# Two units of the first token group's first product by seven products on summed factors, with the factor sums and attention steps placed anew

## The chip, the core and the metric

The kernel runs on one core of a Trainium2 chip. The metric is the device time of one execution in microseconds (us). Engines are named as in the profile: PE multiplies matrices (PEld is its loading of the stationary operand), DVE and ACT work on elements, POOL and SP issue DMAs here. Each engine works through its own instructions in order and waits for others by semaphores.

## The reference

A linear attention with decay, in blocks of 64 positions, over 4 batches, 8 heads, 768 positions and 64 dimensions, feeds a two-layer network. Its result is laid out as 3072 tokens of 512 values.

```python
intra = np.einsum('bhic,bhjc->bhij', qb, kb) * Dmask[None]
intra = np.einsum('bhij,bhjd->bhid', intra, vb)
inter = np.einsum('bhid,bhde->bhie', qb * lam_pow[None], kv_state)
out[:, :, sl] = intra + inter
kv_state = lam_block[None, :, None, None] * kv_state + np.einsum('bhsd,bhse->bhde', kb_dec, vb)
...
h = x @ w_in             # (3072, 512) @ (512, 2048)
g = h - np.tanh(h)
return (g @ w_out).astype(np.float32)   # (3072, 2048) @ (2048, 512)
```

The weights arrive as 64-bit floats. The kernel reads their two 32-bit halves and rounds them to 32 bits itself.

## The kernel before

**Tiling.** Tokens come in six groups g = 0 to 5 of 512 (128 positions of each batch). For each group the kernel makes the attention output (tiles xt, held transposed, in two halves of 256 tokens: half 0 from batches 0 and 1, half 1 from batches 2 and 3), multiplies by w_in ("up"), applies h - tanh(h), and multiplies by w_out ("down"). The hidden width of 2048 is split into four units u = 0 to 3 of 512; `w1[u]` holds the weights of a unit, in four blocks of 128 x 512. The result of a unit, 512 hidden values by 512 tokens, has four quadrants named 11, 12, 21, 22: the first digit is the half of the hidden values, the second the half of the tokens.

**Two ways to make a unit of up.** `up_plain(u, cs)` (line 954) makes quadrants directly: per quadrant 4 x 2 matmul calls, 32 per unit, each quadrant in a PSUM bank of its own (tags ya, yb, z, w), then a tanh on ACT (L971) and a subtraction on DVE (L972). `up(g, u, n)` (line 545) makes product n of a seven-product scheme (that of Strassen in Winograd's form) for the whole unit: 4 calls a product, 28 a unit. The products use sums of weights, made by `sums_in(u)` (four DVE instructions, into `ws[u]`, one into `w1[u]` itself, L261), and sums of tokens, made by `att_sums(g)` (four DVE instructions, L513 to L516). Three banks hold partial results: y takes products 1, 6, 7 and 4 one upon the other, and ACT copies y out after 1 (into bank w, L568), after 6 (L572) and after 7 (L574); w takes product 2; z takes 5 and 3. Group 0 is made by `up_plain` in all four units, groups 1 and on by products (from group 2 on, in a form with a further level).

**The order.** A scheduler at compile time orders the instructions of each engine: earliest in the program first, among those that its own model of times finds ready. `tied(yes, op)` (line 125) pins an instruction behind the one traced just before it on its engine. In between, untied instructions can move ahead of earlier ones that are not ready. PE's plain matmuls are tied in unit 0 and between the parts `att_inter` and `att_intra` (`held["yes"]`). `sums_in` is tied.

**The first 145 us.** Group 0's attention and the weights of the first units come first. Each weight block of 512 KB is loaded by SP, rounded by three ACT instructions (L291 to L293) and two DVE instructions (L295, L296). `weights(n)` sees to it that n blocks are rounded: 16 blocks of w_in, then 16 of w_out, two for each kt = 0 to 7. Then come the four plain units, with the attention of group 1 put between quadrants by the list `turns` (line 1058) in pieces: `att_transpose`, `att_scores`, `att_state`, `att_inter`, `att_intra`, once for batches 0 and 1 (`p0`), once for 2 and 3 (`p1`). `att_intra` waits for a small ACT copy named "seen" (L486) that follows `att_inter`. The loop over kt (line 1081) is the down product of group 0, in seven products of two calls each, into seven banks `acc`, with `sums_out` (sums of w_out, stored to DRAM by POOL for the later groups), `sums_late` and three `sums_in` placed in it. `sums_first(u)` makes two sums of hidden values that this loop reads for unit u = kt // 2. For every third kt the pair of weight tiles of w_out is lent from `ws` (`pair_tiles`, line 249), where no sums of weights are held yet. `powers` (line 108) makes decay factors that attention from group 1 on needs. `first_results` ends group 0; line 1113 begins group 1 with product 1 of its unit 0.

Of the kernel before, what the change touches and what calls it, by code (L numbers as in the profile page):

```python
# [24 lines left out]
def kernel(  # L25
# [32 lines left out]
    nc = tc.nc  # L58
# [190 lines left out]
    def pair_tiles(kt):  # L249

        if kt % 3 == 2:
            return tuple(ws[u].rearrange("p x k c -> p (x k) c")[:, 0:4] for u in (3, 2))
        wt = wst.tile([128, 8, 256], F32, name="wt", tag="w")
        return wt[:, 0:4], wt[:, 4:8]
# [157 lines left out]
    def att_state(g, bs):  # L412
# [17 lines left out]
        for p in range(NP):  # L430
            nc.scalar.activation(mid[:, :, p], old[:, :, p], AF.Copy, scale=fwd[:, p, HALF - 1:HALF])
# [77 lines left out]
    def att_sums(g, bs):  # L509
        x0, x1 = xt[g, 0], xt[g, 1]  # L510
        b11, b21, b12, b22 = x0[:, 0:2], x0[:, 2:4], x1[:, 0:2], x1[:, 2:4]
        tt = xpool.tile([128, 3, 2, HB], F32, name="tt", tag="tt")
        nc.vector.tensor_tensor(tt[:, 0], b12, b11, op=AL.subtract)  # L513
        nc.vector.tensor_tensor(tt[:, 1], b22, tt[:, 0], op=AL.subtract)
        nc.vector.tensor_tensor(b12, b22, b12, op=AL.subtract)
        nc.vector.tensor_tensor(tt[:, 2], b21, tt[:, 1], op=AL.subtract)  # L516
        xt[g] = dict(B11=b11, B21=b21, B22=b22, T1=tt[:, 0], T2=tt[:, 1], T3=b12, T4=tt[:, 2])
# [12 lines left out]
    def product_bank(key, n):  # L530
# [3 lines left out]
        if n == 5 or n == 2 and key[0] == "down":  # L534
            banks[key, "zw"[n == 2]] = bank("zw"[n == 2], "zw"[n == 2], 1)
# [9 lines left out]
    def up(g, u, n):  # L545
# [6 lines left out]
        for m in range(2):  # L552
            for kt in range(2):
                nc.tensor.matmul(out=t[:, m, :], lhsT=wt[:, kt, ts(m, 128)], rhs=x[:, kt, :],  # L554
                                 start=first and m == 0 and kt == 0, stop=kt == 1, skip_group_check=True)
# [10 lines left out]
        if n == 1:  # L566
            w = banks[key, "w"] = bank("w", "w", 1)
# [386 lines left out]
    def up_plain(u, cs):  # L954

        hm = {}
        for c in cs:
            a, t = divmod(c - 11, 10)
            hm[c] = bank("h", ("ya", "yb", "z", "w")[2 * t + a], 1).rearrange("q (m c) -> q m c", m=2)
# [19 lines left out]
    def sums_first(u):  # L979
        g11, g12, g22, s1 = (hidden(0, c)[:, u] for c in (11, 12, 22, "S1"))  # L980
        nc.vector.tensor_tensor(s1, g12, g22, op=AL.add)
        nc.vector.tensor_tensor(g12, g11, g12, op=AL.subtract)
# [42 lines left out]
    for b in (0, 1):  # L1025
# [28 lines left out]
    weights(2 * KI)  # L1054
    every(up_plain(0, (12, 22)))
    sums_first(0)
    p0, p1 = attention(1)
    turns = [(1, 11, 2, ()), (1, 21, 2, ()), (1, 12, 2, ()), (1, 22, 2, ()), (2, 11, 0, ()), (2, 21, 1, p0[0:1]),
             (3, 11, 0, p0[1:3]), (3, 21, 1, p0[3:4]), (2, 12, 1, p0[4:]), (2, 22, 1, p1[0:1]), (3, 12, 1, p1[1:3]),
             (3, 22, 1, ())]  # L1060
    for u, c, n, more in turns:
        every(up_plain(u, (c,)))
        ahead = (u, c) == (2, 12)
        if ahead:
            run(more)
        weights(ready["done"] + n, u > 1)
        if not ahead:
            run(more)
        if c == 22:
            sums_first(u)  # L1070
            if u == 1:
                ready["to"] = len(blocks)
                load(B + 2)
                load_weights(NU * KI + 2)
                load(B + 3)
                load_weights(NU * KI + WAHEAD)
                load(2 * B)
                powers()
    sums_out(0)
    weights(NU * KI + 6, True)  # L1080
    for kt in range(KH):
        down_first(kt, (1, 2))
        if kt == 0:
            run(p1[3:4])
            down_first(kt, (5,))
            run(p1[4:])
        if kt + 1 < KH:
            sums_out(kt + 1)
        sums_late(kt)
        down_first(kt, (4, 7, 6, 3) if kt == 0 else (5, 4, 7, 6, 3) if kt + 1 < KH else (5, 6, 7, 4, 3))  # L1090
        if kt + 3 < KH:
            weights(ready["done"] + 2)
        if kt in (1, 4, 6):
            sums_in((1, 4, 6).index(kt))
# [177 lines left out]
```

## Time and profile before

| | us |
|---|---|
| median of three timed runs | 649.97 |
| the three | 647.11, 649.97, 650.4 |
| the profiled execution | 646.58 |
| its span, first to last instruction | 644.8 |

| engine | busy us | share of the span | instructions |
|---|---|---|---|
| PE | 635.1 | 98% | 6440 |
| DVE | 478.2 | 74% | 948 |
| ACT | 268.0 | 42% | 620 |
| POOL | 229.0 | 36% | 397 |

Lines of the profile name the engine, the line of the kernel, the operation, what is written from what, and shapes. "x16" is a number of instructions; one matmul call in the program is two PE instructions in the trace. A bracket at the end of a line of the timeline is the idle time of that engine just before, with the instruction that ended it. Times are us from the start of the span. In lists of waits the columns are the total, the number and the longest.

### The profile page before, as it was taken

How to read it: one execution, taken by the hardware profiler on the slowest of the kernel's cores; microseconds unless marked ns; L12 is line 12 of the kernel's file. 1: busy time of each engine (PE TensorE's matmuls, PEld its weight loads, DVE VectorE, ACT ScalarE, POOL GpSimd, SP SyncE). 2: the span in 40 equal slices, each digit the busy share in tenths (PEclk: the TensorE clock that was granted, in tenths of full speed). 3: DMA queues.
4: the chain of work that ended last, by engine and by line, in shares of the span. 5: the costliest groups of instructions: out<-in, count | busy, mean ns of one | idle time of the engine just before them, and what ended most of it. 6: DMA issues, size and time to landing. Idle time of an engine off the chain costs nothing.

```text
span 644.8 us, 16628 instructions
## 1 busy us (share of the span) xinstructions
PE 635.1 (98%) x6440; PEld 583.6 (91%) x6440; DVE 478.2 (74%) x948; ACT 268.0 (42%) x620; POOL 229.0 (36%) x397
## 2 busy tenths in 40 slices
PE   8899999999999999999999999999999999999998
PEld 6788878888888999998999998999998899998997
DVE  4577597785888877579968579987668987467953
ACT  3799576503432422345331337233245332334310
POOL 0000355735443454411455430355321254521261
PEclk9999999999999999999999999999999999999999
DMA  9999988969765999884889976798883477732384
GB/s 216 233 244 232 294 265 268 348 187 267 210 164 126 288 278 298 224 188 112 230 236 304 280 203 157 184 276 249 253 198 80 138 234 241 248 105 77 100 296 145
DMA packets 166190, 139.80 MB, mean 217 GB/s; under 512 B 136864, under 2 KB 138016, under 8 KB 166112
## 3 DMA queue, kind: packets, MB, share of 16 engines
q0 software_dynamic: 31792, 104.62, 50.0%
q1 hardware_dynamic: 134176, 34.12, 25.9%
q8 instruction: 51, 0.84, 0.5%
q14 instruction: 27, 0.22, 0.1%
q10 hardware_dynamic: 144, 0.00, 0.0%
HBM read 111.94 MB, written 26.74 MB: 215 GB/s over the span
## 4 chain that ended last, share of the span: by engine, by line
PE 65%; issue 18%; POOL 8%; DVE 3%; DMA 3%; ACT 2%; SPq 2%; POOLq 0%; DVEq 0%
PE plain L849 10%; PE acc L993 7%; PE h L964 7%; PE y L906 6%; PE y L697 6%; PE zw L906 4%; PE y L554 4%; POOL wb L795 4%; PE z L697 3%; PE zs L619 2%; PE z L554 2%; PE y L619 2%; POOL wb L792 2%; PE op L501 1%; PE w L697 1%
## 5 line engine op out<-in xcount | busy, mean ns | idle before, releaser
L795 POOL DMA_DIRECT2D wb<-fine x133 | 71.8, 541 | 157.5 <-PE plain L849 107.8
L849 PE MATMUL plain<-wb,g 128*128 128x256 f32 x416 | 96.0, 381 | 0.0
L849 PEld LDWEIGHTS plain<-wb,g 128*128 128x128 f32 x416 | 77.5, 190 | 10.4
L964 PE MATMUL h<-xt,w 128*128 128x256 f32 x256 | 57.9, 382 | 1.8 <-DVE w L296 1.8
L798 POOL DMA_DIRECT2D wb<-factors x64 | 34.6, 541 | 69.2 <-PE z L697 47.9
L910 ACT ACTIVATE q<-y 128x128 f32<-128x128 f32 x76 | 21.1, 278 | 86.1 <-PE y L906 85.0
L964 PEld LDWEIGHTS h<-xt,w 128*128 128x128 f32 x256 | 47.7, 190 | 9.0 <-DVE w L296 2.0
L906 PE MATMUL y<-wb,g 128*128 128x128 f32 x336 | 44.8, 278 | 0.0
L792 POOL DMA_DIRECT2D wb<-fine_in x60 | 32.6, 545 | 29.3 <-PE z L697 11.0
L600 ACT ACTIVATE th<-g 128x512 f32<-128x512 f32 x48 | 29.5, 628 | 29.0 <-DVE g L625 28.9
L906 PEld LDWEIGHTS y<-wb,g 128*128 128x128 f32 x336 | 40.7, 192 | 0.7
L688 ACT ACTIVATE g<-y 128x512 f32<-128x512 f32 x24 | 14.3, 597 | 63.1 <-PE y L697 63.1
L404 ACT ACTIVATE k_nat<-k_nat,mask 128x64 f32<-128x64 f32 (+1 forms) x128 | 35.1, 338 | 0.6 <-DMA k_nat<-in_k_dram 0.6
L993 PE MATMUL acc<-wt,g 128*128 128x256 f32 x144 | 32.9, 380 | 0.2 <-DVE g L972 0.2
L601 DVE TENSOR_TENSOR g<-g,th 128x512 f32<-128x512 f32 x48 | 32.2, 687 | 0.4
L697 PE MATMUL z<-tt,wb 128*128 128x128 f32 x256 | 31.9, 275 | 0.0
L993 PEld LDWEIGHTS acc<-wt,g 128*128 128x128 f32 x144 | 27.2, 190 | 4.3 <-DVE g L972 0.6
L619 PE MATMUL y<-xt,w 128*128 128x256 f32 x128 | 30.3, 379 | 0.0
L619 PE MATMUL zs<-xt,ws 128*128 128x256 f32 x128 | 30.2, 379 | 0.0
L906 PE MATMUL zw<-wb,g 128*128 128x128 f32 x224 | 30.2, 278 | 0.0
L697 PEld LDWEIGHTS z<-tt,wb 128*128 128x128 f32 x256 | 30.2, 192 | 0.0
L292 ACT ACTIVATE r<-raw 128x512 int16<-128x512 uint32 x32 | 25.0, 782 | 8.3 <-DMA raw<-in_moe_w_out_dram 3.8
(236 smaller groups left out, 1476.2 us busy)
## 6 DMA issues: line engine op xcount, KB each, us to landing
wb<-fine POOLq DMA_DIRECT2D x133, 256.0 KB, 4.0
wb<-factors POOLq DMA_DIRECT2D x64, 256.0 KB, 4.3
wb<-fine_in POOLq DMA_DIRECT2D x60, 256.0 KB, 4.8
v_nat<-in_v_dram SPq DMA_DIRECT2D x24, 256.0 KB, 5.3
raw<-in_moe_w_out_dram POOLq DMA_DIRECT2D x12, 512.0 KB, 5.7
k_nat<-in_k_dram SPq DMA_DIRECT2D x20, 256.0 KB, 4.6
fine<-wt POOLq DMA_DIRECT2D x17, 256.0 KB, 3.4
raw<-in_moe_w_in_dram SPq DMA_DIRECT2D x8, 512.0 KB, 5.2
```

The source lines that it names most:

```text
L404: tc.keep_in_program_order(nc.scalar.activation(k_h, k_h, AF.Copy, scale=mask[0:rows, h % 2, h // 2, HALF - 1:HALF]))
L554: nc.tensor.matmul(out=t[:, m, :], lhsT=wt[:, kt, ts(m, 128)], rhs=x[:, kt, :], start=first and m == 0 and kt == 0, stop=kt == 1, skip_gro ...
L601: nc.vector.tensor_tensor(dst(c), src, th, op=AL.subtract)
L619: nc.tensor.matmul(out=t[:, m, :], lhsT=wt[:, kt, ts(m, 128)], rhs=x[:, kt, :], start=False, stop=kt == 1, skip_group_check=True)
L697: nc.tensor.matmul(out=dst[:, ts(u, 128)], lhsT=a, rhs=b, start=(x in (1, 5) or x == 2 and not filled) and u == 0, stop=True, skip_group_c ...
L792: nc.gpsimd.dma_start(out=t.rearrange("p m c -> p (m c)"), in_=fine_in[INNER.index(n_[1]), (5, 6, 3).index(x_)].rearrange("p u c -> p (u c)"))
L795: nc.gpsimd.dma_start(out=t.rearrange("p m c -> p (m c)"), in_=fine[TWICE.index(n_), SUB.index(x_)].rearrange("p u c -> p (u c)"))
L798: nc.gpsimd.dma_start(out=t, in_=factors[XAT[FACT[n_][1]]][:, 2 * x_:2 * x_ + 2, :])
L849: tied(held["yes"], nc.tensor.matmul(out=t[:, m, :], lhsT=a[:, u, kt, ts(m, 128)], rhs=wb[:, kt, :], start=first and u == 0 and m == 0 and ...
L906: tied(held["yes"], nc.tensor.matmul(out=dst, lhsT=a[:, u, :], rhs=wb[:, ts(u, 128)], start=x in (1, 2) and u == 0, stop=u == NU - 1, skip ...
L964: tied(u == 0 or held["yes"], nc.tensor.matmul(out=hm[c][:, m, :], lhsT=w1[u][:, i, a, ts(m, 128)], rhs=xt[0, t][:, i, :], start=m == 0 an ...
L993: tied(held["yes"], nc.tensor.matmul(out=acc[n][:, r, :], lhsT=a[:, ts(r, 128)], rhs=b, start=kt == 0 and r == 0, stop=kt == KH - 1, skip_ ...
```

## The change

In group 0, units 1 and 2 are made by seven products; units 0 and 3 stay plain. Around it:

- `att_sums(0)` runs before unit 0's second two quadrants. Since the plain units still read the tokens, its third sum T3 is written to a free place among the hidden sums (unit 3's part of S1), and unit 3's `sums_first` moves from its last quadrant to kt = 3.
- `sums_in(1)` and `sums_in(2)` move from kt = 4 and 6 to before and into unit 1, and `sums_in(0)` from kt = 1 to kt = 6. The pair tiles lent are now those of units 3 and 0.
- Unit 1's products come one after the other (1, 5, 2, 6, 7, 4, 3), all tied on PE, its banks z and w taken from the four of attention. Unit 2's products take turns with unit 3's quadrants and the pieces of group 1's attention. Unit 3's quadrants use banks w and yb only.
- The number of w_out blocks rounded before the loop over kt is five in place of six; the sixth comes after the second `att_intra`. `powers` comes after unit 2's product 5.
- The scaling copies of the attention state (L431) of group 2 are tied, and so are the two instructions of `sums_first` but for unit 0.

The hidden sums S1 and 12 of units 1 and 2, made by `sums_first` before, are made at the end of product 3 in `up`.

```diff
-            return tuple(ws[u].rearrange("p x k c -> p (x k) c")[:, 0:4] for u in (3, 2))
+            return tuple(ws[u].rearrange("p x k c -> p (x k) c")[:, 0:4] for u in (3, 0))
...
-            nc.scalar.activation(mid[:, :, p], old[:, :, p], AF.Copy, scale=fwd[:, p, HALF - 1:HALF])
+            tied(g == GI, nc.scalar.activation(mid[:, :, p], old[:, :, p], AF.Copy, scale=fwd[:, p, HALF - 1:HALF]))
...
-        nc.vector.tensor_tensor(b12, b22, b12, op=AL.subtract)
+        t3 = b12 if g > 0 else hidden(0, "S1")[:, NU - 1]
+        nc.vector.tensor_tensor(t3, b22, b12, op=AL.subtract)
...
-            banks[key, "zw"[n == 2]] = bank("zw"[n == 2], "zw"[n == 2], 1)
+            spare = key == ("up", 0, 1)
+            banks[key, "zw"[n == 2]] = bank("zw"[n == 2], "att" if spare else "zw"[n == 2], 4 if spare else 1)
...
-                nc.tensor.matmul(out=t[:, m, :], lhsT=wt[:, kt, ts(m, 128)], rhs=x[:, kt, :],
-                                 start=first and m == 0 and kt == 0, stop=kt == 1, skip_group_check=True)
+                tied(held["yes"], nc.tensor.matmul(
+                    out=t[:, m, :], lhsT=wt[:, kt, ts(m, 128)], rhs=x[:, kt, :], start=first and m == 0 and kt == 0,
+                    stop=kt == 1, skip_group_check=True))
...
-            w = banks[key, "w"] = bank("w", "w", 1)
+            w = banks[key, "w"] = bank("w", *(("att", 4) if key == ("up", 0, 1) else ("w", 1)))
...
-            hm[c] = bank("h", ("ya", "yb", "z", "w")[2 * t + a], 1).rearrange("q (m c) -> q m c", m=2)
+            tag = ("w", "yb")[a] if u == NU - 1 else ("ya", "yb", "z", "w")[2 * t + a]
+            hm[c] = bank("h", tag, 1).rearrange("q (m c) -> q m c", m=2)
...
-        nc.vector.tensor_tensor(s1, g12, g22, op=AL.add)
-        nc.vector.tensor_tensor(g12, g11, g12, op=AL.subtract)
+        tied(u > 0, nc.vector.tensor_tensor(s1, g12, g22, op=AL.add))
+        tied(u > 0, nc.vector.tensor_tensor(g12, g11, g12, op=AL.subtract))
...
+    att_sums(0, None)
     every(up_plain(0, (12, 22)))
+    sums_in(1)
     sums_first(0)
     p0, p1 = attention(1)
-    turns = [(1, 11, 2, ()), (1, 21, 2, ()), (1, 12, 2, ()), (1, 22, 2, ()), (2, 11, 0, ()), (2, 21, 1, p0[0:1]),
-             (3, 11, 0, p0[1:3]), (3, 21, 1, p0[3:4]), (2, 12, 1, p0[4:]), (2, 22, 1, p1[0:1]), (3, 12, 1, p1[1:3]),
-             (3, 22, 1, ())]
...
+    held["yes"] = True
+    for n in (1, 5, 2, 6, 7, 4, 3):
+        up(0, 1, n)
+        weights(ready["done"] + 1 + (n == 1))
+        if n == 2:
+            sums_in(2)
...
+    turns = [(2, 1, 0, ()), (2, 5, 0, ()), (2, 2, 0, ()), (2, 6, 0, p0[0:1]), (3, 11, 0, p0[1:3]), (2, 7, 1, ()),
+             (3, 21, 0, p0[3:4]), (2, 4, 1, p0[4:]), (3, 12, 1, p1[0:1]), (2, 3, 1, p1[1:3]), (3, 22, 1, ())]
...
+        if (u, x) == (2, 5):
+            powers()
+        if (u, x) == (2, 2):
+            held["yes"] = False
     sums_out(0)
-    weights(NU * KI + 6, True)
+    weights(NU * KI + 4, True)
     for kt in range(KH):
         down_first(kt, (1, 2))
         if kt == 0:
             run(p1[3:4])
             down_first(kt, (5,))
             run(p1[4:])
+            weights(NU * KI + 6, True)
...
-        if kt in (1, 4, 6):
-            sums_in((1, 4, 6).index(kt))
+        if kt == 3:
+            sums_first(NU - 1)
+        if kt == 6:
+            sums_in(0)
```

More of the change, by code (lines that the diff above doesn't have):

```diff
@@ L514, in att_sums @@
         nc.vector.tensor_tensor(tt[:, 1], b22, tt[:, 0], op=AL.subtract)
-        nc.vector.tensor_tensor(b12, b22, b12, op=AL.subtract)
+        t3 = b12 if g > 0 else hidden(0, "S1")[:, NU - 1]
+        nc.vector.tensor_tensor(t3, b22, b12, op=AL.subtract)
         nc.vector.tensor_tensor(tt[:, 2], b21, tt[:, 1], op=AL.subtract)
-        xt[g] = dict(B11=b11, B21=b21, B22=b22, T1=tt[:, 0], T2=tt[:, 1], T3=b12, T4=tt[:, 2])
+        xt[g] = dict(B11=b11, B21=b21, B22=b22, T1=tt[:, 0], T2=tt[:, 1], T3=t3, T4=tt[:, 2])
     def attention(g):
@@ L1054 @@
     weights(2 * KI)
+    att_sums(0, None)
     every(up_plain(0, (12, 22)))
+    sums_in(1)
     sums_first(0)
     p0, p1 = attention(1)
-    turns = [(1, 11, 2, ()), (1, 21, 2, ()), (1, 12, 2, ()), (1, 22, 2, ()), (2, 11, 0, ()), (2, 21, 1, p0[0:1]),
-             (3, 11, 0, p0[1:3]), (3, 21, 1, p0[3:4]), (2, 12, 1, p0[4:]), (2, 22, 1, p1[0:1]), (3, 12, 1, p1[1:3]),
-             (3, 22, 1, ())]
-    for u, c, n, more in turns:
-        every(up_plain(u, (c,)))
-        ahead = (u, c) == (2, 12)
+    held["yes"] = True
[4 more added lines that the diff above has]
+            sums_in(2)
+    ready["to"] = len(blocks)
+    load(B + 2)
+    load_weights(NU * KI + 2)
+    load(B + 3)
+    load_weights(NU * KI + WAHEAD)
+    load(2 * B)
+    turns = [(2, 1, 0, ()), (2, 5, 0, ()), (2, 2, 0, ()), (2, 6, 0, p0[0:1]), (3, 11, 0, p0[1:3]), (2, 7, 1, ()),
+             (3, 21, 0, p0[3:4]), (2, 4, 1, p0[4:]), (3, 12, 1, p1[0:1]), (2, 3, 1, p1[1:3]), (3, 22, 1, ())]
+    for u, x, n, more in turns:
+        if u == 2:
+            up(0, u, x)
+        else:
+            every(up_plain(u, (x,)))
+        ahead = (u, x) == (2, 4)
         if ahead:
             run(more)
-        weights(ready["done"] + n, u > 1)
+        weights(ready["done"] + n, True)
         if not ahead:
             run(more)
[L1069 to L1078, printed above, removed]
+        if (u, x) == (2, 5):
+            powers()
+        if (u, x) == (2, 2):
+            held["yes"] = False
     sums_out(0)
-    weights(NU * KI + 6, True)
+    weights(NU * KI + 4, True)
     for kt in range(KH):
@@ L1091 @@
         if kt + 3 < KH:
-            weights(ready["done"] + 2)
-        if kt in (1, 4, 6):
-            sums_in((1, 4, 6).index(kt))
+            weights(ready["done"] + 2, kt == 0)
+        if kt == 3:
+            sums_first(NU - 1)
+        if kt == 6:
+            sums_in(0)
     first_results()
```

## The prediction

> **What bounds the kernel now.** First the page's busy shares, then the table of busy time by stage, cut at the places where the change works.
>
> ```profile
> PE 635.1 (98%) x6440; PEld 583.6 (91%) x6440; DVE 478.2 (74%) x948; ACT 268.0 (42%) x620; POOL 229.0 (36%) x397
> ```
>
> ```profile
> 30.20:38.90 8.70, 8.68 (x40) 7.68 (x41) 5.61 (x11) 8.70 (x16) 0.00 (x0) 1.00 0.83 240
> 38.90:52.90 14.00, 14.00 (x67) 12.32 (x66) 10.63 (x20) 13.84 (x24) 0.00 (x0) 1.00 1.03 231
> ...
> 87.40:94.00 6.60, 6.41 (x32) 5.11 (x28) 6.50 (x16) 4.40 (x7) 3.48 (x6) 1.00 0.86 241
> 94.00:98.30 4.30, 3.42 (x134) 2.78 (x133) 3.09 (x8) 2.59 (x7) 2.93 (x5) 1.00 1.04 389
> 98.30:143.20 44.90, 44.90 (x211) 39.55 (x209) 34.66 (x74) 18.89 (x31) 24.85 (x39) 1.00 0.85 273
> ```
>
> The columns are the stretch, its length, busy time of PE, PEld, DVE, ACT and POOL, granted clock, DMA share and GB/s. PE is never idle from 30 to 92 us and from 98 us on, so a matmul removed there shortens the kernel by its own time and a wait added there lengthens it. The second line is the second unit (u = 1): ACT, busy with rounding weights, is full too (13.84 of 14.00), so whatever PE must get from ACT there queues. The two lines before the last hold the only PE gap, 1.1 us, and the list of PE's waits names it:
>
> ```profile
> PE op L501 <- ACT seen L486: 0.9, 1, 0.9
> PE acc L993 <- DVE g L972: 0.2, 1, 0.2
> ```
>
> In order of time, ACT and DVE around the second unit, and then the first hand-over of a product bank in group 1:
>
> ```profile
> 39.86 1.05 ACT L971 ACTIVATE th<-h 128x512 f32<-128x512 f32 x2
> ...
> 43.91 0.58 ACT L971 ACTIVATE th<-h 128x512 f32<-128x512 f32 x1
> ```
>
> ```profile
> 40.47 1.29 DVE L972 TENSOR_TENSOR g<-h,th 128x512 f32<-128x512 f32 x2
> ```
>
> ```profile
> 147.63 1.89 PE L554 MATMUL y<-tt,ws 128*128 128x256 f32 x8
> ...
> 149.56 0.60 ACT L572 ACTIVATE g<-y 128x512 f32<-128x512 f32 x1 [1.07 <-PE y L554]
> ...
> 150.21 3.32 PEld L554 LDWEIGHTS y<-xt,w 128*128 128x128 f32 x16 [0.23 <-ACT g L572]
> ```
>
> **What is removed.** A matmul call is two instructions in the trace. A plain unit has 32 calls, a unit in products 28, so two units lose 8 calls or 16 instructions. The chain gives 16 plain instructions as 3.46 us: **-3.46 us** of PE, where PE has no slack.
>
> The tie on L431 takes four state copies of group 2 (1.25 us from 95.80) from in front of "seen" (96.95), for which PE waits 0.9 us. Without them "seen" could start at 95.95, when inter has ended and the rounding before it is through. I take **-0.9**; the ends are 0 (something else stands there) and -1.1, all of the gap.
>
> **The second unit's waits.** Its seven products run tied, so PE can do nothing else in a wait.
>
> (a) Product 5 needs S1, and the first factor sum is tied behind the last DVE instruction traced, the L972 of unit 0's quadrant 22. PE ends unit 0 at 30.22 + 40 x 0.2178 (29.62 us for 136) = 38.9 and product 1 at 40.6. The L972 pair ends at 41.76, S1 takes 0.6 to 0.7 more: 42.4, a wait of 1.8. If the two tanh ran at once (38.95), S1 would be there at 41.4: 0.8. If rounding gets in front too, one more L296 makes it 2.5. I take **+1.8**, the order that the trace shows.
>
> (b) Products 6, 7 and 4 use one bank, y, and ACT copies y out between them, with no other product in the gap. Group 1 shows the least price: its matmuls end at 149.52, the copy runs 0.60, the next starts at 150.21: 0.69. There ACT was free. In the second unit the four tanh start 1.5, 0.9, 0.9 and 0.1 us after their quadrants end (43.91 against 42.4, and so on), 0.85 on average; with the copy 1.5. Behind a whole block of rounding (1.82 at its closest pitch) it is 2.5. PE slowed by one wait comes nearer to ACT's order, so I take 1.1 each, between 0.69 and 1.5: **+2.2** (1.4 to 5.0).
>
> (c) Product 2 waits for the copy of y to w, but product 5 and wait (a) lie between, over 3 us: 0 (up to 0.7).
>
> **The third unit** (u = 2) is taken in turns with unit 3's quadrants and attention, so 6, 7 and 4 have 3.46 us and more between them. Its products 1, 5, 2 have only 1.73 us for the copy to w, when ACT still rounds the last blocks (ended at 55.4, now some 2 us later): **+0.3** (0 to 0.8). Quadrant 11 of unit 3 takes bank w, free after tanh and subtraction (0.59 + 0.69), with product 6 and the transposes (1.73 + 1.75) in between: 0; with 2 us more of queue it would wait.
>
> **Inter to intra of group 1.** Between the first pair's two halves stands product 4 with 1.73 us in place of a quadrant with 3.46. In group 2 the same distance, 8 matmuls between inter at 207.88 and intra at 210.90, shows no wait; in the first case here "seen" ended 1.7 us after inter. **+0.2** (0 to 1.0).
>
> **ACT and DVE.** Per unit in products: three copies at 0.58 to 0.60, +1.8 us of ACT, and two additions at 0.69, +1.4 of DVE. The token sums of group 0 add four at 0.69: 2.7, in a stretch with 8.70 - 5.61 = 3.1 us of idle DVE; were that gone, T1 would come late and product 5 with it. Factor sums of units 1 and 2 (four at 0.69 each) come from the loop over kt to before 56 us, 5.5 us against 3.4 of idle DVE in the second unit: DVE runs some 3 to 4 us behind, and catches up between 60 and 80 us, where it is idle 7.75 of 20. In front of the second inter the third unit's last product brings one DVE instruction more, one rounded block (1.1 of DVE, some 2 of ACT) goes behind intra, and unit 3's sums leave (1.4). **+0.3**, from 0 to 1.7, what the third unit saves: the filler that PE loses there.
>
> **What costs nothing, and why.** The attention banks that the second unit borrows are not wanted before the transposes at 59.5. The powers (1.7 of ACT, then 1.7 of DVE) move behind product 5 of the third unit and end near 60.5, needed after the transposes at about 63; without that margin qd and the scores would be late. The loads on SP behind them keep their order and come about 2 us later: q and k went out from 47.5 on and are needed at 61. The first POOL issues (from 66.6) wait for DVE's rounding and move with it; kt = 0 needs their sources, not the stores. Unit 0's sums move to kt = 6, where 134.32 to 137 already held such a set, while S1 is wanted at 144.76; unit 3's sums move to kt = 3 and are wanted at kt = 6, near 131. The sixth block is wanted at kt = 2, 106.8, and would be rounded by 101. T3's place and the pair's other tile change no instruction. The loop over kt loses 5.5 us of DVE with PE full already: nothing.
>
> **Sum.** -3.46 - 0.9 + 1.8 + 2.2 + 0.3 + 0.2 + 0.3 = **+0.4 us**: no change. Low end: -3.46 - 1.1 + 0.8 + 1.4 = -2.4. With everything at its worst +8; four fifths of that is not likely at once, and for the range I keep +4.8, rival 2 below. The profiled execution took 646.58 (span 644.8 and 1.8 around it), under all three timed runs (647.11, 649.97, 650.4) and 3.4 under their median. A new median can fall anywhere among these, so I set the sum on the mean of the four, 648.5: **648.9**. What a measurement of this kernel can tell from no change is about 0.5%, 3.2 us, the spread of those runs.
>
> **Rivals.**
> 1. *The waits stay at their least* (a 0.8, b 1.4, "seen" gone): 648.5 - 2.4 = 646.1, and with (a) covered wholly 645.3. For it: copies come before later blocks in program order. Against: the tanh, with that same precedence, were late three times of four.
> 2. *ACT's queue decides, and it is slower.* Every y copy stands behind a full block, 2.5 each, S1 at 2.5, w copies 0.8: -3.46 + 5.0 + 2.5 + 0.8 = +4.8 with "seen" no better: 653.3. It decides once the waits of both units pass 3.46 + 3.2 = 6.7 us. For it: 13.84 of 14.00. Against: those blocks are not due for 10 us.
> 3. *The second inter takes the gain back.* From 82.7 to 92.9 the chain runs through DVE without a gap. If it stays as long, the third unit's 1.73 is lost: 650.6, still no change.
> 4. *PE slows after short pauses.* Three stops in 16 us: were the granted clock halved there, 12.1 us of matmuls (56 x 0.2165) would take 24.2, and the time be 661. The rows speak against: from 6 to 12 us PE was busy 1.23, 1.60 and 1.31 of each 2 us and the clock stayed at 1.00, as it did from 94 to 98. [...]
>
> **Chances.** My sum 0.50; rival 1 0.16; rival 2 0.22; rival 3 0.09, of which 0.02 ends slower; rival 4 0.03. Faster is rival 1: 0.16. Slower: 0.22 + 0.02 + 0.03 = 0.27. Within: 0.57. The range for eight in ten: from 645.3 (rival 1's far end) to 653.3 (rival 2's own time); it leaves out the upper half of rival 2, rival 4 and little else. My sum's own range is 646.1 to 651.5.
>
> **What would show it.** PE instructions 6424. Between products 1 and 5 of the second unit a PE gap near 1.8 ended by DVE's factor sum; two gaps near 1.1 ended by the copies of y; that unit ending 1.5 to 2.5 us later than 52.9. The third unit without gaps over 0.5. No wait for "seen" in the second pair, and the state copies of group 2 after it. No new gap from 98 on, with clock 1.00 throughout. I am wrong if the scheduler puts S1 or the copies elsewhere than the trace before suggests, or if the plan after 143 us changes enough to open gaps where there are none.

## The result and the profile after

| | before | after |
|---|---|---|
| median, us | 649.95 | 656.65 |
| the runs, us | 650.4, 649.97, 647.11, 649.93 | 656.18, 657.12, 657.85, 654.18 |
| the profiled execution (span), us | 646.58 (644.8) | 656.18 (654.4) |

The ratio is 1.0111 (95% interval 1.0083 to 1.0139): slower, and above the predicted range (645.3 to 653.3). The profiled execution of before lies under all its timed runs, so the two profiles differ by more (9.6 us) than the medians (6.7 us).

The first table answers where the time went. It was put together from the starts of PE's bursts in the two traces, each counted from PE's first instruction (1.36 us after the start of the span in both).

```
start of                          before     after    after minus before
first pair, scores                 63.61      66.94      +3.33
second pair, inter                 92.69      93.57      +0.88
second pair, intra                 95.79      96.13      +0.34
group 1 (the loop over kt is done) 141.88     146.79     +4.91
scores of group 3's first pair     299.17     305.26     +6.09
inter after it                     308.30     316.13     +7.83
scores of its second pair          323.65     331.28     +7.63
inter after it                     332.12     341.79     +9.67
end                                643.40     653.05     +9.65
```

Up to the second intra, where the change works, 0.34 us is lost; it is 1.2 when one counts that before has by then also done four matmul instructions (0.87 us) of the down product that after still has to do. The larger part of the loss comes behind it: 4.6 us in the loop over kt (3.7 by the same count), 1.2 in small steps up to 299, and 1.7 and 2.0 in two short stretches of group 3's attention, over 200 us after the last changed unit.

The busy line of the page after, and the longest of PE's waits from 30 us on:

```profile
PE 634.1 (97%) x6424; PEld 580.0 (89%) x6424; DVE 482.5 (74%) x956; ACT 270.7 (41%) x626; POOL 228.9 (35%) x397
```

```profile
PE kv L437 <- issue: 3.3, 3, 1.7
PE acc L997 <- DVE g L1005: 2.5, 1, 2.5
PE z L556 <- DVE ws L261: 1.6, 1, 1.6
...
PE y L556 <- ACT g L575: 1.3, 1, 1.3
PE y L556 <- ACT g L577: 0.9, 1, 0.9
PE acc L997 <- DVE g L1004: 0.6, 1, 0.6
```

PE has the 16 instructions fewer, and "seen" is no longer among the waits. The third, fourth and fifth line are the second unit, the second and the last the loop. The first was not foreseen at all: stops in the state update of attention (kv), for which the profile shows no releaser ("issue").

The second unit in PE's timeline (start, duration, instructions, idle time before):

```profile
39.39 1.89 PE L556 MATMUL y<-xt,w 128*128 128x256 f32 x8
42.88 1.99 PE L556 MATMUL z<-tt,ws 128*128 128x256 f32 x8 [1.59 <-DVE ws L261]
44.71 1.89 PE L556 MATMUL w<-xt,w 128*128 128x256 f32 x8
46.43 1.89 PE L556 MATMUL y<-tt,ws 128*128 128x256 f32 x8
49.62 1.99 PE L556 MATMUL y<-gS,w 128*128 128x256 f32 x8 [1.29 <-ACT g L575]
52.54 1.99 PE L556 MATMUL y<-tt,w 128*128 128x256 f32 x8 [0.93 <-ACT g L577]
```

Products without a stop start 1.73 us apart. With that, the three stops cost 1.76, 1.46 and 1.19 us from start to start, 4.4 in all; each costs about 0.2 more than its idle time.

The loop over kt, on DVE, between 125 and 129 us, and what ACT waited for just before:

```profile
125.86 1.00 DVE L295 TENSOR_SCALAR wt<-wt 128x512 uint32<-128x512 uint32 x2 [3.12 <-ACT wt L291]
126.77 1.29 DVE L296 CUSTOM_DVE_ANT_0 wt<-wt,r 128x1024 uint16<-128x1024 uint16 x2
127.98 0.68 DVE L985 TENSOR_TENSOR gS<-g,g 128x512 f32<-128x512 f32 x1
128.58 0.42 DVE L1005 TENSOR_TENSOR g<-g,g 128x256 f32<-128x256 f32 x1
```

```profile
124.53 0.79 ACT L292 ACTIVATE r<-raw 128x512 int16<-128x512 uint32 x1 [6.03 <-DMA raw<-in_moe_w_out_dram]
```

PE waits for the last of those DVE lines. In front of it stand unit 3's tied sum (L985) and two rounded blocks; in front of them DVE waits 3.1 us for ACT, and ACT 6.0 us for a weight block. POOL issued the load of that block, with another, at 117.06; the pair that stands there in before went out at 111.34. The load alone is not shown to be what held ACT: L291, which follows at 125.18, writes a tile whose store to DRAM (factors<-wt, issued at 120.03) landed at 125.17. Which of the two would have held it without the other is not shown. How the loads fell behind is seen in the windows of before and of after (columns as in the prediction's table: the last is GB/s):

```profile
75.00:98.00 23.00, 21.93 (x395) 18.44 (x397) 18.18 (x39) 16.98 (x33) 11.66 (x19) 1.00 0.90 288
...
125.00:140.00 15.00, 15.00 (x71) 13.20 (x70) 11.32 (x23) 2.90 (x5) 7.96 (x12) 1.00 0.84 254
```

```profile
75.00:98.00 23.00, 22.62 (x432) 18.96 (x434) 18.06 (x39) 15.00 (x29) 9.13 (x15) 1.00 0.82 227
...
125.00:140.00 15.00, 12.54 (x59) 10.72 (x58) 11.59 (x26) 6.02 (x10) 12.30 (x19) 1.00 0.94 301
```

Between 75 and 98 us the DMA engines move 61 GB/s less, 1.4 MB in 23 us; the bytes come later, at 98 to 112 (325 GB/s for 252) and at 125 to 140. A smaller shortfall lies ahead of this stretch: 215 GB/s for 230 from 30 to 56 us, 235 for 268 from 56 to 75. The rounding shows the same: its last instruction on the first block of w_out starts at 65.6 us before and at 76.2 after, that on the sixth at 93.8 and 102.9. In the last third of the loop SP begins a chain of loads for the attention of groups 2 and 3 that runs with hardly a pause to 290 us. It begins later, and its first tile takes longer (of before, then of after):

```profile
129.86 8.91 SPq L151 DMA_DIRECT2D q_blk<-in_q_dram  x16
```

```profile
134.16 12.48 SPq L151 DMA_DIRECT2D q_blk<-in_q_dram  x16
```

Last, one of the two stops in group 3's attention:

```profile
333.62 0.64 PE L437 MATMUL kv<-v_nat,k_nat 64*64 64x64 f32 x30
335.96 0.82 PE L437 MATMUL kv<-v_nat,k_nat 64*64 64x64 f32 x34 [1.70 <-issue]
```

In the trace a transfer of 16,384 bytes on the queue called "instruction" begins at 333.30, 2.7 us before PE goes on; at the other stop (310.01) one begins at 307.32. Counted over all of PE's records in the trace, which are its 12,848 matmuls and weight loads and 225 semaphore and drain instructions, the stop stands behind record 6338 in the one case and 5570 in the other: both are 256 times a whole number plus 194. The page has 51 packets of 0.84 MB in all on that queue, and 51 is also how many such places there are among the 13,073 records. Below, such a place is called a boundary and such a transfer a fetch. That PE waited there for its own instructions is the author's reading of these counts and times; the profile itself gives no releaser. The change takes 32 matmuls and weight loads out of PE's stream and puts four semaphore instructions in: the state update in which the first stop falls starts at record 5466 in place of 5494, and every boundary from group 2 on is moved by 28 records against the work. The two stops cost 1.6 and 1.9 us from start to start.

### The profile page after: what moved, and what is told of

It reads as the page before. It is cut to its first block, busy times and chain, and to the rows that moved or that the text cites. A ratio compares the mean times of both kernels' runs of the same rounds, so it can differ in the third digit from the quotient of the medians.

```text
span 654.4 us, 16615 instructions
## 1 busy us (share of the span) xinstructions
PE 634.1 (97%) x6424; PEld 580.0 (89%) x6424; DVE 482.5 (74%) x956; ACT 270.7 (41%) x626; POOL 228.9 (35%) x397
## 4 chain that ended last, share of the span: by engine, by line
PE 52%; issue 20%; POOL 8%; DMA 7%; DVE 5%; ACT 5%; SPq 2%; POOLq 0%; ACTq 0%
PE plain L852 9%; PE y L556 6%; PE y L700 5%; PE y L909 4%; POOL wb L798 4%; PE zw L909 3%; PE z L556 3%; PE acc L997 3%; PE z L700 3%; DMA factors<-wt 2%; PE zs L622 2%; PE y L622 2%; POOL wb L795 2%; DMA q_blk<-in_q_dram 2%; PE h L968 1%
## 5 line engine op out<-in xcount | busy, mean ns | idle before, releaser
L216 POOL DMA_DIRECT2D raw<-in_moe_w_out_dram x12 | 6.9, 576 | 88.2 <-ACT r L293 86.3
L968 PE MATMUL h<-xt,w 128*128 128x256 f32 x128 | 29.7, 384 | 1.9 <-DVE w L296 1.9
```

The costliest lines, as they stand in the source:

```text
L968: tied(u == 0 or held["yes"], nc.tensor.matmul(out=hm[c][:, m, :], lhsT=w1[u][:, i, a, ts(m, 128)], rhs=xt[0, t][:, i, :], start=m == 0 an ...
```

## The experiments

Four causes were open: the w_out rounding one turn later (below *late rounding*, theory L in the expectations), unit 3's sums tied in the loop (*sums in the loop*, rival S), the second unit's own stops with the delay that they hand on (rival U), and the moved fetch boundaries (*fetch*, theory F). All ratios are against runs of the kernel before on the same chip, with their 95% interval. "At group 1" and the like are differences of the profiled execution to that of before, from the table's milestones.

**1. One block rounded one turn earlier.** Product 6 of unit 2 gets the rounding that the change took from there. PE's order of instructions stays that of after.

```diff
-    turns = [(2, 1, 0, ()), (2, 5, 0, ()), (2, 2, 0, ()), (2, 6, 0, p0[0:1]), (3, 11, 0, p0[1:3]), (2, 7, 1, ()),
+    turns = [(2, 1, 0, ()), (2, 5, 0, ()), (2, 2, 0, ()), (2, 6, 1, p0[0:1]), (3, 11, 0, p0[1:3]), (2, 7, 1, ()),
```

> Edit: in the changed kernel the first block of w_out is rounded behind product 6 of the third unit, so that every later block comes one turn earlier and the sixth before the loop over kt, as before. Theory L (late rounding): in the changed kernel the first five blocks of w_out end their rounding 4 to 11 us later than before, so loads and stores of the same size have less time, the loop over kt waits 3.1 us, the last block ends 4.3 us later, SP's block loads for group 2 start 4.3 us later, and the two kv waits of 3.1 us near 335 us follow. It expects about 650.5 us against 656.65: no PE wait from 98 to 148 us, SP's first block load near 130, no kv waits. Rival S (order on DVE: unit 3's two sums, tied in front of L1005 at kt = 3, hold up the loop): the 2.5 us wait stays, no better than 654. Rival U (the second unit's own waits, 3.8 us, and the delay they hand on): within 1.5 us of 656.65.

650.22 us against 647.29: 1.0044 (1.0029 to 1.0060), where the change had 1.0111. From 75 to 98 us the DMA engines move 258 GB/s (227 in after, 288 in before). The 2.46 us wait is gone and group 1 starts at +2.02 instead of +4.91. What is left in the waits, beside the second unit's three:

```profile
PE kv L437 <- issue: 2.2, 1, 2.2
...
PE acc L997 <- DVE g L1004: 0.6, 1, 0.6
```

That this stop stayed was not expected. It stands behind record 6338, as in after, and costs more than its length: +1.83 before it, +6.00 behind it. The windows of PE around it (busy, granted clock, DMA share, GB/s) show why:

```profile
328.00:331.00 3.00, 0.75 (x43) 1.00 0.95 272
331.00:334.00 3.00, 3.00 (x43) 0.51 0.21 39
```

The clock was halved for 3.41 us after it (0.51 in the second window). So late rounding is the larger part of the loss, and the loop's wait hangs on it.

**2. Unit 3's sums before the loop.** Four DVE instructions change their place.

```diff
+    sums_first(NU - 1)
     sums_out(0)
...
-        if kt == 3:
-            sums_first(NU - 1)
```

> Edit: unit 3's two sums of hidden values go back from kt = 3 to before the loop over kt. Theory L: 655.5 to 657.5, the loop's waits stay near 3 us. Rival S: the 2.5 us wait of the loop goes and with it the later start of SP's loads: 651 to 654. Rival U: as L.

653.99 against 647.29: 1.0110 (1.0072 to 1.0148), no better than the change. The 2.46 us wait does go (1.1 is left) and group 1 starts at +2.62. But the gain is given back: ACT waits for the late loads of group 3's attention, and PE behind it, and the profile ends at +7.7 without any stop in the state update.

```profile
ACT k_nat L404 <- DMA k_nat<-in_k_dram: 5.3, 1, 5.3
```

In before this wait was 0.6 us, in after 2.2. As far as this one execution shows, the sums decide whether the delay is felt in the loop or later, not how long it is. PE's stream has the same matmuls and weight loads as in after, and yet the fetch stops are not there.

**3. The second unit plain.** Unit 1 by quadrants again, its sums of weights at kt = 4; all else as after.

```diff
-    sums_in(1)
     sums_first(0)
...
-    for n in (1, 5, 2, 6, 7, 4, 3):
-        up(0, 1, n)
-        weights(ready["done"] + 1 + (n == 1))
-        if n == 2:
+    for c in (11, 21, 12, 22):
+        every(up_plain(1, (c,)))
+        weights(ready["done"] + 2)
+        if c == 21:
             sums_in(2)
+    sums_first(1)
...
+        if kt == 4:
+            sums_in(1)
```

> Edit: the second unit is made by plain quadrants again, its factor sums at kt = 4; the third unit stays in seven products. By the traces the three waits of the second unit (1.6 + 1.3 + 0.9 = 3.8) go and 1.7 of matmuls come back: 2.1 less. Theory L: rounding of w_out is some 2 us earlier than in the changed kernel and still 2 to 9 later than before: 652 to 655, with part of the loop's and the kv waits left. Rival U: about 650 or lower, with neither loop waits nor kv waits.

649.61 against 647.29: 1.0033 (1.0017 to 1.0049). In the profiled execution, the longest of its ten (652.83), the second intra starts at -1.79; then the loop waits 0.9 and 3.4 us, in the longer of these waits the clock fell to half for 6.8 us (the mean granted clock of the execution is 0.992), and group 1 starts at +6.85. The third unit alone is therefore a gain up to the loop, which the loop takes away in this execution. The time is what rival U had expected (about 650), the waits in the loop are those of theory L.

**4. The kernel before with only the rounding late.** Its PE stream, and so its fetch boundaries, are those of before.

```diff
-             ... (2, 11, 0, ()), (2, 21, 1, p0[0:1]),
+             ... (2, 11, 0, ()), (2, 21, 0, p0[0:1]),
...
-    weights(NU * KI + 6, True)
+    weights(NU * KI + 4, True)
...
             run(p1[4:])
+            weights(NU * KI + 6, True)
...
-            weights(ready["done"] + 2)
+            weights(ready["done"] + 2, kt == 0)
```

> Edit: the kernel before, with nothing but the blocks of w_out one turn later (five before the loop over kt, the sixth behind the second intra). Theory L: 654 to 657, with waits in the loop over kt and kv waits near 330 us that the kernel before doesn't have. Rivals S and U: 650, since neither unit 3's sums nor the second unit is touched.

651.69 against 647.29: 1.0061 (1.0038 to 1.0084). Late rounding alone makes the kernel before slower by 4.4 us, less than the 654 to 657 that theory L expected, and without the waits in the loop and the stops that it expected. (The last line of the edit, which pins the rounding behind kt = 0 in order, belongs to the change too.) In its profile little of it is in the loop (group 1 at +0.38); the loads on SP run up to some 4 us late, and it ends at +3.7 by these waits of PE and of ACT:

```profile
PE zs L619 <- DVE zs L610: 1.3, 2, 1.1
...
PE plain L849 <- ACT plain L838: 0.7, 1, 0.7
PE acc L993 <- DVE g L1000: 0.7, 1, 0.7
...
ACT k_nat L404 <- DMA k_nat<-in_k_dram: 3.8, 1, 3.8
```

**5. After, with 32 PE records put back.** In the warm-up at the start (`idle`), which ends long before the changed work, one matmul of 128 columns gives way to nine of 16. That puts the boundaries from group 2 on within four records of where they were before (the state update of the first stop starts at record 5498; before had 5494).

```diff
-    for _ in range(8):
+    for _ in range(7):
         nc.tensor.matmul(out=idle[:, 0:128], ...)
+    for _ in range(9):
+        nc.tensor.matmul(out=idle[:, 0:16], lhsT=ident, rhs=ident[:, 0:16], start=True, stop=True)
```

> Edit: the changed kernel with eight more matmul calls, of 16 columns, among the idle ones at the very start, where PE waits for data anyhow; the order of everything else is the same. The change took 8 calls, which are 32 PE instructions with their weight loads, out of the stream; this puts the count back, so that every later PE instruction has the place in the stream that it had before. Theory F (fetch): in the changed kernel PE stops for 1.7 us in the middle of two kv bursts, each time while a 16 KB transfer on the instruction queue begins (307.3 and 333.3 us), so the stops are PE waiting for its instructions, and where they fall follows from the count. It expects both kv stops gone, 3 to 4 us less than the changed kernel: ratio to the kernel before about 1.005 to 1.007 in place of 1.011. Rival D (the kv stops wait for late data: decayed keys or values behind SP's late loads): stops and ratio as in the changed kernel.

658.49 against 648.81: 1.0159 (1.0114 to 1.0204), a miss. The stop at 336 us goes, as fetch has it, and of that at 310 us 0.54 is left, behind record 5570 as in after, but the late loads come out in their place: ACT waits 4.2 us for k_nat (2.2 in after), PE 1.7 for the sums that follow, and the profile ends at +8.5. Another 1.8 us were lost at the start, where the clock, once full, was halved again for 3.41 us (the mean granted clock is 0.997). That this came of the edit is not shown: in experiment 3, whose warm-up is that of before, the clock was also halved again (from 7.7 to 11.1 us), and 0.8 us was lost there. So the two losses are no sum here; why is not shown.

**6. Before, with its 32 warm-up records taken out.** The converse: PE's stream of before, shifted about as the change shifts it (the state update of the first stop starts at record 5463; after has 5466).

```diff
-    for _ in range(8):
-        nc.tensor.matmul(out=idle[:, 0:128], lhsT=ident, rhs=ident, start=True, stop=True)
```

> Edit: the kernel before without its eight idle calls at the start, which are 32 PE instructions: the rest of the stream then has the places that it has in the changed kernel. Theory F: kv stops of about 1.7 us near 300 and 325 us appear, and 2 to 4 us more than the kernel before (ratio 1.003 to 1.006), part of it perhaps from an unwarmed start. Rival D: no kv stops, ratio within 0.2% of 1, but for what the start costs before 30 us.

651.0 against 648.81: 1.0037 (1.0013 to 1.0061). Without any of the change, the stop of after appears, behind record 6337, with a fetch that begins 2.6 us earlier:

```profile
329.63 0.64 PE L435 MATMUL kv<-v_nat,k_nat 64*64 64x64 f32 x31
332.26 0.82 PE L435 MATMUL kv<-v_nat,k_nat 64*64 64x64 f32 x33 [1.99 <-issue]
```

It cost 3.96 us there, with the clock halved for 3.41 us behind it. The rest of the 7.5 us by which this profile is longer than that of before lies ahead of it: the first quadrant began 1.5 us late, and 2.1 came between there and the stop. So the stop needs nothing of the change's work. That the count of instructions alone makes it is not shown, since the edit moved the start in time as well.

**7. Sums early, units 1 and 2 interleaved.** The version meant to remove the second unit's stops: the rounding of experiment 1, the padding of experiment 5, `sums_in(1)` ahead of unit 0's last quadrants, and unit 2's first products put between those of unit 1.

```diff
-    every(up_plain(0, (12, 22)))
     sums_in(1)
+    every(up_plain(0, (12, 22)))
...
-    for n in (1, 5, 2, 6, 7, 4, 3):
-        up(0, 1, n)
+    for u, n in ((1, 1), (1, 5), (1, 2), (1, 6), (2, 1), (1, 7), (2, 5), (1, 4), (2, 2), (1, 3)):
+        up(0, u, n)
...
+    powers()
+    turns = [(2, 6, 1, p0[0:1]), (3, 11, 0, p0[1:3]), ...
```

> Edit: the changed kernel with rounding one turn earlier (as in the first experiment), the count of PE instructions put back, the second unit's factor sums traced before unit 0's last two quadrants (so S1 is not tied behind their subtractions), and products 1, 5 and 2 of the third unit put between 6, 7, 4 and 3 of the second. My theory: the second unit's three stops (1.76 + 1.46 + 1.19 us by start times) go, and with them what the saving was lost to: 1 to 4 us faster than the kernel before, ratio 0.994 to 0.998. Rival U2 (ACT and DVE cannot serve products in that stretch in any order): stops of 2 us or more remain there or move to the third unit, ratio 1.000 to 1.006.

654.57 against 648.81: 1.0079 (1.0049 to 1.0109), a miss. The stops of the second unit are gone: the first inter is 6.5 us later than in before, and 6.0 of these were there already when up began. They were lost at the start, where with the short warm-up matmuls the clock rose to full at 19.3 us (6.6 in before), and a fetch stop of 1.7 us with 3.41 us of half clock behind it fell into the first pair's intra.

**8. The third unit alone.** Experiment 3 with the rounding of experiment 1 and four calls more (16 records) in the warm-up, so that later boundaries are within one record of where they were before.

```diff
-    for _ in range(8):
+    for _ in range(7):
...
+    for _ in range(5):
+        nc.tensor.matmul(out=idle[:, 0:16], lhsT=ident, rhs=ident[:, 0:16], start=True, stop=True)
...
(unit 1 by quadrants and (2, 6, 1, p0[0:1]), as above)
```

> Edit: the changed kernel with the second unit in plain quadrants, rounding one turn earlier, and the count of PE instructions put back. My theory: without the second unit's stops the third unit's saving (1.73) and the missing wait for the copy named seen (0.9) show: 1 to 2.5 us faster than the kernel before, ratio 0.996 to 0.999. Rival (the loop over kt and the later loads lose as much whatever the second unit does): ratio 1.001 or more.

649.7 against 648.81: 1.0004 (0.9987 to 1.0022), between the two expectations. The profiled execution is ahead by 1.9 us at the second inter and 1.2 at group 1, and loses it all by 324 us (+3.9) to late loads: ACT waits 5.1 us for k_nat.

**9 and 10. Before and after with cheap loads.** The q and k tiles of groups 2 to 5 come by one DMA each. The edit leaves out the transposition that the sixteen DMAs of a tile made: the same bytes land in other places, the output from group 2 on is another, and only the time is read.

```diff
-                for p in range(NP):
-                    for c in range(4):
-                        blk = src[b, 2 * p + c // 2, ts(g, BLK), ts(c % 2, 32)]
-                        tc.keep_in_program_order(
-                            nc.sync.dma_start(out=x[ts(c, 32), p], in_=blk.rearrange("(r t) a -> t r a", t=32)))
+                tc.keep_in_program_order(nc.sync.dma_start(
+                    out=x.rearrange("s p r a -> s (p r a)").rearrange("s (h d) -> s h d", h=H),
+                    in_=src[b, :, ts(g, BLK), :].rearrange("h s d -> s h d")))
```

> Edit: the kernel before with each tile of transposed blocks of q and k (groups 2 to 5) loaded by one DMA in the natural layout in place of sixteen with 128-byte runs. The same bytes, but the values land in the wrong places, so attention from group 2 on computes something else; its time is read, not its output. Theory SP (SP's loads, 9 to 12 us a tile, run just at PE's pace, so that whatever makes them later or slower is paid by ACT waiting for k_nat and by PE behind it near 230 to 335 us): no ACT wait for k_nat, the runs lie closer together, 0.1 to 0.5% faster than the kernel before. Rival (loads hidden anyway): within 0.1%.

652.92 against 647.76: 1.0082 (1.0040 to 1.0124). A miss.

> Edit: the same cheap loads in the changed kernel, wrong in the same way. Theory SP: no ACT wait for k_nat, and of the 9.7 us between the two profiles the 4.9 up to the start of group 1 stay, with the kv stops (fetch) on top, 1.7 us each: ratio to the kernel before 1.004 to 1.010. If the kv stops vanish here though the PE stream is the same instruction for instruction, they waited for loads and theory F falls. Rival (loads hidden anyway): 1.011 as the changed kernel.

661.02 against 647.76: 1.0203 (1.0168 to 1.0237). A miss too. In both the wait for k_nat is gone from ACT, as expected, but fetch stops come out at new places (columns: the total, the number and the longest). Of the kernel before with cheap loads, then of after:

```profile
PE op L499 <- issue: 2.7, 1, 2.7
PE kv L435 <- issue: 1.4, 1, 1.4
```

```profile
PE kv L435 <- issue: 3.6, 1, 3.6
PE y L907 <- issue: 2.1, 1, 2.1
```

All four stand at 193 or 194 beyond a whole number of 256 records, each with a fetch that begins 2.4 to 2.6 us before PE goes on; three of them (2.7, 3.6 and 2.1 us) were followed by a halved clock (the mean granted clock is 0.997 in experiment 9 and 0.992 in 10). The stops behind records 5570 and 6338 are not there, although PE's stream is that of after. What was expected beforehand counts this against fetch in its simple form, in which the count alone makes the stops. What is left of it is what these traces show: the stops stand at boundaries, but not at the same ones each time. In after the fetches for the two stops begin when PE has run 5427 and 6240 records, so that 143 and 98 were left to run: 1.2 and 0.8 us, estimated from the 2.09 us that 256 such records take in before (from 325.01), while the transfers took 1.25 and 1.17. Here they begin at 5308 and 6122, some 118 records earlier. That the start of the fetch decides is the author's reading; what delays one is not shown.

**11. Experiment 7, its padding moved.** The warm-up is as in before; eight short calls (32 records) stand behind `first_results`, where the clock is full. PE has 6440 instructions, as before.

```diff
     first_results()
+    pad = bank("pad", "att", 4)
+    for _ in range(8):
+        tc.keep_in_program_order(nc.tensor.matmul(
+            out=pad[:, 0:16], lhsT=ident, rhs=ident[:, 0:16], start=True, stop=True, skip_group_check=True))
```

> Edit: as the experiment with early factor sums and interleaved products, but with the idle calls at the start as they were (the short ones there left PE's clock halved up to 19 us), and the eight short calls that put the count of PE instructions back placed behind the first group's results. My theory: no stops in the second unit, no half clock at the start; 2 to 4 us ahead of the kernel before at the start of group 1, part of it lost to SP's loads: ratio 0.994 to 0.999. Rival U2: 1.000 to 1.006.

646.06 against 647.76: 0.9978 (0.9959 to 0.9997), 10 runs against 21. This version is a quarter of a per cent faster than before, with an interval that ends just under 1, and by its ratio faster than after (1.0111). No wait of the second unit is above 0.2 us and none is in the loop; of the fetch stops this is left:

```profile
PE kv L437 <- issue: 0.4, 1, 0.4
```

Its DMA windows have lost most of the shortfall of after, and by 125 us the DMA engines have moved more than in before (268 against 261 GB/s from 0 to 125 us), so that no more than 211 is left for 125 to 140:

```profile
75.00:98.00 23.00, 22.52 (x396) 19.32 (x387) 20.59 (x44) 14.04 (x29) 13.08 (x20) 1.00 0.93 267
...
125.00:140.00 15.00, 15.00 (x72) 13.19 (x71) 8.88 (x19) 0.60 (x1) 5.96 (x9) 1.00 0.71 211
```

The second intra starts at -3.65 and group 1 at -2.40; by 231 us the profiled execution is level with that of before, which is itself short among its runs.

**12. Experiment 8, its padding moved.** Four short calls behind `first_results`, the warm-up as before.

```diff
+    for _ in range(4):
+        tc.keep_in_program_order(nc.tensor.matmul(
+            out=pad[:, 0:16], lhsT=ident, rhs=ident[:, 0:16], start=True, stop=True, skip_group_check=True))
```

> Edit: as the experiment with the third unit alone in products, with the start as it was and four short calls behind the first group's results. My theory: 1 to 2 us ahead at the start of group 1 and up to 3 lost behind it to SP's loads: ratio 0.997 to 1.001. Were the loads hidden, 0.996.

647.19 against 647.76: 0.9989 (0.9972 to 1.0006), no difference that can be told. One wait of 0.9 us is left in the loop.

## Why the prediction was wrong

**The steps that it costed were near.** PE's 16 instructions went (-3.46), and so did the wait for "seen". Wait (a) was put at 1.8 and took 1.76. Wait (b) was put at 2.2 and took 2.65: the copy after product 6 came nearer to the upper end of its bounds (1.46), the one after 7 to the value taken (1.19). The third unit's w copy (0.3) and the inter to intra of the first pair (0.2) cost nothing. At the second intra the kernel after stands at +0.34, and before has by then done four matmul instructions (0.87 us) of the down product that after has not; so the stretch cost +1.2 where the sum said +0.4. With the terms as measured, and 0.5 for a wait for ACT in the second pair's scores, -3.46 - 0.9 + 1.76 + 2.65 + 0.5 = +0.55; the other 0.65 stands against the 0.3 that was put for DVE and ACT. Of it 0.44 lies in unit 0, ahead of the second unit: PE gets the last block that it waits for there at 30.66 in place of 30.22, and on DVE a token sum (L514, from 29.10) stands right in front of that block's last instruction (29.91 in place of 29.47). The rest is not taken apart. (The list of PE's waits in the prediction leaves out two lines, 0.8 us at that block and 0.4 near 618 us; PE of before is not quite "never idle" from 98 us on. Nothing hangs on it.)

**The step that failed is "What costs nothing".** Three of its sentences failed, in what they said or in what they left out.

- "The sixth block is wanted at kt = 2, 106.8, and would be rounded by 101." The time itself was 2.6 us off (DVE ended that block at 103.6) and did no harm: the work that needs it began at 108.2 without a wait. What was wrong is what it was taken for: one block rounded one turn later was looked at as one block with one due time. But POOL's load of a raw block waits for ACT to have rounded an earlier one (86.3 of the 88.2 us that POOL sat idle before these loads end with L293), so the whole chain of w_out's loads stands behind each block, and the DMA engines moved 227 GB/s where they had moved 288. The load that came some 6 us later (117.06 for 111.34) is that of a block for kt = 6, not kt = 2. Experiments 1 (1.0111 to 1.0044) and 4 (1.0061 by this alone) show that this is the larger part of the loss.
- "The loop over kt loses 5.5 us of DVE with PE full already: nothing." PE was not slowed by DVE's work but by its order: unit 3's sum, tied, and the accumulation after it stood behind rounding that waited for ACT. The wait was 2.46 and 0.6. Experiment 2 removes the wait, but not the loss, since the loads that caused it are as late as before.
- "The loads on SP behind them keep their order and come about 2 us later." That was said for those of group 1; the chain that begins late in the loop was not looked at. It began 4.3 us late, and in experiments 2, 4, 5 and 8 ACT's wait for them (3.8 to 5.3 us, 0.6 before) was what PE came to wait for.

**Not in the prediction at all** was the place of the fetch boundaries. "No new gap from 98 on" did not hold; the new gaps of 1.4 and 1.7 us lie at boundaries that the change had moved by 28 records. Experiment 6 shows such a stop in a kernel that has nothing else of the change, and experiments 2 and 10 show that the moved boundaries do not bring it each time. In the profile of after the two stops with all that goes with them took 1.7 and 2.0 us.

**The rivals.** Rivals 1 and 3 did not occur: the second unit's waits were not at their least, and between the second pair's state update and its inter PE gained 1.3 us. Rival 2's time (653.3) was passed, but not by its mechanism: ACT's copies came sooner than behind a full block each. Rival 4 did not decide the time of the profiled execution of after: its three stops of 0.9 to 1.6 us within 12 us left the clock at 1.00. It came nearer than these rows look, though. The prediction argued from gaps of 0.4 to 0.8 us in each 2; in experiments 1, 3, 6, 7, 9 and 10 single stops of 1.7 us and more were followed by one or two stretches of 3.41 us at half clock, each of which costs some 1.7 us where PE is full (an estimate: half of 3.41). The longest of the three stops, 1.59 us, lay not far under the 1.7 of experiment 7; the stop of 1.70 in after was not followed by half clock.

**What stays open.** How the loss of the runs that were not profiled is shared between late loads and fetch stops: they take each other's place (experiments 2, 5, 8, 10), so no sum of parts can be given. What makes a fetch begin 118 records later in one kernel than in another was not tried. Nor is the part of the DMA shortfall taken apart that experiment 1 leaves (258 GB/s for 288).

## What to carry to other kernels

When work that frees a load's buffer is moved, the cost is not the due time of that piece but that of every load queued behind it: read the GB/s of the stretch before (here 288, and 227 after) and ask what the DMA engines will do instead. Here a change in the number of PE's instructions moved its boundaries by 28 records against all that followed, and two stops over 200 us after the last changed unit took 1.7 and 2.0 us with what goes with them, so such a change is best compared with its count made up as well, by a few short calls where the clock is full. A wait seen in one place can be moved without being removed; only the end tells.

## What the runs showed of the hardware

- PE stopped with no releaser in the profile for 1.4 to 3.6 us (1.6 to 3.8 from start to start), each time at 193 or 194 beyond a multiple of 256 records (semaphore instructions counted in), 2.4 to 2.8 us after a 16,384-byte transfer on the instruction queue began. All the stops over 1 us but one stood in attention's 64x64 matmuls, where 64 scores and 64 state updates with their weight loads, 256 records, pass in 2.09 us (before, from 325.01). (The one at a 128x128 matmul is experiment 10's second.)
- The granted clock fell to half for 3.41 us with stops of 1.7 us (experiment 7), 2.0 (6 and 10), 2.1 (10), 2.2 (1), 2.7 (9) and 3.6 (10), and for twice as long with the wait of 3.4 in experiment 3, but not with stops of 1.4 and 1.7 in after, 1.4 in experiment 9, or the loop's 2.46. The mean granted clock of these executions is 0.997 in experiments 1, 6, 7 and 9, 0.992 in 3 and 10, and 0.999 in after. No run was made to find what divides the stops that were followed by half clock from the others.
- The start differs between kernels with the same warm-up, and only one execution of each kernel was profiled: the clock was full from 6.60 us on in before, where the first four transpose instructions took 1.12 us (at 5.00) and four like them 0.66 (at 8.81), and from 4.98 on in after, where both took 0.65 or 0.66. With nine short matmuls (16 columns) for one long (128) in the warm-up, 1.8 and 6.0 us were lost at the start (experiments 5 and 7), with five for one nothing (8): in experiment 5 the clock was full from 5.1 us on and halved again from 8.5 to 11.9; in experiment 7 it rose at 19.3 us. But experiment 3, with the warm-up of before, lost 0.8 us in the way of experiment 5, so the short matmuls are not shown to be the cause.
